# The stored expert weights: the two halves of each piece laid apart in DRAM

## The chip, the cores and the metric

The kernel runs on one core of a Trainium2 chip. The metric is device time in microseconds (us) of one execution. Five instruction streams take part: TensorE (PE, with its weight loads as PEld), VectorE (DVE), ScalarE (ACT), GpSimd (POOL) and SyncE (SP), which issues most DMA transfers. All transfers run on the same 16 DMA engines of the core, fed from several queues: q1 holds what SP issues, q10 what ACT issues, q0 the indirect transfers that POOL issues.

## The reference

```python
def _attn_ref(q, k, v, f_logit):        # (4, 8, 768, 48) each
    f = 1.0 / (1.0 + np.exp(-f_logit))
    for t in range(S):
        state = f[:, :, t, :, None] * state + np.einsum('bhd,bhe->bhde', k[:, :, t], v[:, :, t])
        y[:, :, t] = np.einsum('bhd,bhde->bhe', q[:, :, t], state)

def _moe_ref(x, w_in, w_out, alpha):    # x: 3072 x 384, hidden width 2048
    h = x @ w_in
    g = np.maximum(h, 0.0) + alpha * np.minimum(h, 0.0)
    return g @ w_out

def _moe2_ref(x, w_gate, w1, w2):       # 8 experts, 384 -> 1024 -> 384
    logits = x @ w_gate
    order = np.argsort(-logits.flatten())
    for idx in order:                   # greedy; every expert takes exactly 384 tokens
        tok, e = int(idx) // E, int(idx) % E
        if assigned[tok] >= 0 or counts[e] >= cap:
            continue
        assigned[tok] = e; counts[e] += 1
    for e in range(E):
        out[assigned == e] = np.maximum(x[assigned == e] @ w1[e], 0.0) @ w2[e]
```

The three run one after the other on 3072 tokens of width 384.

## The kernel before

**Matmuls in two parts.** Each fp32 operand of the two feed-forward layers is split into a rounded high part (fp32r) and the remainder, also fp32r. A product is three matmuls: high by low, low by high, high by high.

**Stages.** Attention runs in 24 chunks of 128 tokens; the first feed-forward layer in eight blocks of 384 tokens, each three chunks behind the attention. A block's result, three 128 x 384 tiles, is stored to the DRAM tensor `x2d` (SP issues these stores, ACT those of the last block). Then comes routing: for each expert in turn a search on DVE and PE finds the threshold, `lists` makes the list of its 384 tokens, `gather` (line 1442) reads their rows from `x2d` with three indirect DMAs on POOL, PE transposes the rows, and `expert` (line 1456) computes. The search for expert p+1 is woven into the matmuls of expert p.

**The expert weights.** `convert` (line 1398) runs beside the first feed-forward layer. For each expert e and each of eight pieces i it loads 128 x 768 floats of `w1` or `w2`, and for each half u of the piece ACT writes the high part and DVE the remainder into a tile `w` of 128 x 2 x 384 (name `wtwo`, three buffers), which SP stores to the DRAM tensor `wd`: 128 stores of 384 KB. `expert_weights` (line 1425) loads an expert's eight pieces when the search has named it, one DMA of 768 KB each (128 partitions x 1536 floats), into the SBUF space of the first layer's weights. Loads for one expert go to the `win` tiles, for the next to the `wo` tiles.

**What sets the order.** All of this is recorded as operations in a `Plan`, and a list scheduler (`schedule`, line 326) places them: it takes the operation that can start earliest by its own costs, breaks ties by priority, and emits every engine's instructions in that order. An operation waits for the operations whose memory regions overlap with its own. A region is a box of partitions and byte ranges; `region` (line 574) keeps at most 32 separate runs and merges the finest dimension of what is over:

```python
    while outer and count > 32:
        s, n = outer.pop(0)
        span += s * (n - 1)
        count //= n
```

`touch` (line 252) makes a write depend on earlier writes that overlap, for `x2d`, the output and `wd`. In idle time of PE the scheduler sets matmuls of constants (line 1667), which keep PE's clock up.

**Names in the rows.** Recorded operations have line 210 (feed-forward activations also 230), the loads of `wd` line 1440. `early` are tiles of attention and conversion, `common` gathered rows and block results, `late` the routing's small tiles, `weights` the SBUF weights, `rounded` split activations. `common<-x2d,late` is a gather, `x2d<-common` a block's store, `wd<-early` a store of a split half, `weights<-wd` a load of a piece, `bank<-ident,common` a transpose of gathered rows.

Of the kernel before, what the change touches and what calls it, by code (L numbers as in the profile page):

```python
# [9 lines left out]
F32 = mybir.dt.float32  # L10
# [10 lines left out]
N, DM, DF = B * S, H * D, 2048  # L21
E, FE = 8, 1024
# [609 lines left out]
class Kernel:  # L632
# [765 lines left out]
    def convert(self):  # L1398

        nc = self.nc  # L1400
        for e in range(E):
            for i in range(8):
                if i < 4:
                    t = self.cv.tile([128, KD, 256], F32, name="wraw", bufs=2)
                    src = self.w1[e].rearrange("(c q) f -> q c f", q=128)[:, :, i * 256:(i + 1) * 256]
                    flat = t.rearrange("p c f -> p (c f)")
                else:
                    t = self.cv.tile([128, 2, DM], F32, name="wraw", bufs=2)
                    src = self.w2[e].rearrange("(c q) d -> q c d", q=128)[:, 2 * i - 8:2 * i - 6, :]
                    flat = t.rearrange("p u d -> p (u d)")  # L1410
                nc.sync.dma_start(t, src)
                for u in range(2):
                    w = self.cv.tile([128, 2, DM], F32R, name="wtwo", bufs=3)
                    part = flat[:, u * DM:(u + 1) * DM]
                    nc.scalar.activation(w[:, 0], part, AF.Copy)
                    nc.vector.tensor_tensor(w[:, 1], part, w[:, 0].bitcast(F32), OP.subtract)
                    nc.sync.dma_start(self.wd[e, i, :, u], w.bitcast(F32))

    def expert_tiles(self, p):

# [4 lines left out]
    def expert_weights(self, p, ei):  # L1425

        ts = self.expert_tiles(p)

        def source(i, r):
            return self.wd[ds(r, 1), i].rearrange("o q u s d -> q (o u) s d")  # L1430

        if not self.plan:
            r = self.nc.sync.value_load(ei[0:1, 0:1], min_val=0, max_val=E - 1)
            for i, t in enumerate(ts):
                self.nc.sync.dma_start(t.bitcast(F32), source(i, r))
            return
        reg = []
        get = self.plan.add(("sync",), lambda e, b: reg.append(e.value_load(b(ei[0:1, 0:1]), min_val=0, max_val=E - 1)), [], [ei], 100.0)
        for i, t in enumerate(ts):
            self.plan.add(("sync",), lambda e, b, i=i, t=t: e.dma_start(b(t.bitcast(F32)), source(i, reg[0])), [t], [self.wd], 60.0, 128 * 1536 * 4, [get])  # L1440

    def gather(self, idx):
        xg = [self.gw.tile([128, DM], F32, name="g", bufs=3) for a in range(3)]
# [192 lines left out]
    def main(self, ctx):  # L1636
        tc = self.tc
        with ExitStack() as es:
            cp = es.enter_context(tc.tile_pool(name="consts", bufs=1))
            dp = es.enter_context(tc.tile_pool(name="dram", bufs=1, space=DRAM))  # L1640
            self.x2d = dp.tile([N, DM], F32, name="x2d")
            self.wd = dp.tile([E, 8, 128, 2, 2, DM], F32, name="wd")
            self.banks = 3
            self.wide = False
            self.urgent, self.slack = 0.0, SLACK
            with ExitStack() as e1:
                pp = e1.enter_context(tc.tile_pool(name="psum", bufs=1, space=PSUM))
                banks = [pp.tile([128, 512], F32, name=f"bank{i}") for i in range(8)]
                plan = self.nc = self.plan = Plan(tc, banks, (self.x2d.tensor.name, self.out.tensor.name, self.wd.tensor.name))
                self.pp = plan.group(None)  # L1650
                self.xp = plan.group(plan.arena("rounded"))
                self.gw = plan.group(plan.arena("common"))
                early = plan.arena("early")
                self.ap = plan.group(early)
                self.sp = plan.group(early, self.ap)
                self.cv = plan.group(early, self.ap)
                raw = [plan.arena(f"raw{n}") for n in reversed(range(NF))][::-1]
                self.raw = [plan.group(a) for a in raw]
                self.wp = [plan.group(plan.arena(f"weights{n}", "right", raw[:n + 1])) for n in range(NF)]
                over = raw + [early]  # L1660
                self.tail = plan.group(plan.arena("hidden", over=over))
                late = plan.arena("late", over=over)
                self.rp = plan.group(late, bufs=2)
                self.ep = plan.group(late, self.rp)
                self.record(cp)
                idle = self.ones[:, None, :].to_broadcast([128, 4, 128])
                plan.filler = lambda e, k: e.matmul(banks[k], self.ones, idle, start=True, stop=True)
                plan.emit()
            self.nc, self.plan, self.wide = tc.nc, None, False
            bad = tc.nc.values_load(self.bad[0:1, 0:1], min_val=0, max_val=1)  # L1670
            with tc.If(bad > 0):
                self.general()
# [169 lines left out]
```

## Time and profile before

| | |
|---|---|
| median of 3 runs | 859.87 us (858.52 to 860.99) |
| the profiled execution | 861.39 us, its span 859.5 us |
| mean granted TensorE clock over the span | 0.984 |
| PE busy | 825.2 us (96%) |
| PEld, DVE, ACT, POOL busy | 88%, 66%, 41%, 14% |
| moved by DMA | 172.60 MB, mean 201 GB/s |
| `wd` stores | 128 of 384 KB, 3.6 us to landing (median) |
| `wd` loads | 64 of 768 KB, 5.6 us to landing (median) |

The span is the time from the first to the last instruction of the profiled execution. What lies around it, 861.39 - 859.5 = 1.9 us, is start and end. [...] PE is busy nearly throughout, so an average says little; the stretches have to be read one by one, looking for those in which PE stands still and what it stands still for.

### The profile page before, as it was taken

Reading aid. Unit: us, or ns where it says so; the run is one execution under the profiler, and the core shown is the slowest. Engines: PE = TensorE matmul, PEld = TensorE weight load, DVE = VectorE, ACT = ScalarE, POOL = GpSimd, SP = SyncE. Lnnn points to the kernel's source line nnn. Section 1 sums busy time; section 2 is a strip of 40 time slices with the busy share of each in tenths; the row PEclk is TensorE's granted clock in tenths of the full one; section 3 lists DMA queues with packets and bytes.
Section 4 is the critical chain, followed back from the end, with each engine's and each line's share of the span. In section 5 each row is a group of like instructions: output and inputs, shape, how many; then the busy total and the mean of one; then the engine's idle time right before and its main releaser. Section 6 shows DMA issues by size and latency. Waiting matters only on the chain. (4 is left out here: it accounts for less than half of the span.)

```text
span 859.5 us, 16037 instructions
## 1 busy us (share of the span) xinstructions
PE 825.2 (96%) x6123; PEld 760.2 (88%) x6123; DVE 563.2 (66%) x1301; ACT 349.8 (41%) x742; POOL 121.5 (14%) x112
## 2 busy tenths in 40 slices
PE   7899899999999999999999999998899999999995
PEld 3678789999999999999999999986788898999995
DVE  6898996966966966966866645555667557453220
ACT  2477676455455455455454433410112222212220
POOL 3232410200200200300100001000102212201211
PEclk9899999999999999999999999999899999999998
DMA  8995215789788788898887610007548865777400
GB/s 175 277 251 162 48 29 140 160 281 288 207 286 271 217 281 261 213 308 245 233 266 271 230 76 28 1 10 311 186 175 339 340 248 194 266 278 260 163 27 32
DMA packets 92789, 172.60 MB, mean 201 GB/s; under 512 B 31672, under 2 KB 61376, under 8 KB 92704
## 3 DMA queue, kind: packets, MB, share of 16 engines
q1 hardware_dynamic: 89056, 161.45, 59.1%
q0 software_dynamic: 3072, 9.44, 3.1%
q8 instruction: 50, 0.82, 0.4%
q10 hardware_dynamic: 576, 0.60, 0.2%
q14 instruction: 35, 0.29, 0.1%
HBM read 111.69 MB, written 59.77 MB: 199 GB/s over the span
## 5 line engine op out<-in xcount | busy, mean ns | idle before, releaser
L210 PE MATMUL bank<-rounded,weights 128*128 128x384 f32 (+1 forms) x1740 | 355.5, 345 | 1.4 <-POOL weights L210 1.1
L210 PE MATMUL bank<-weights,rounded 128*128 128x392 f32 (+1 forms) x1620 | 324.0, 344 | 1.5 <-DVE weights L210 0.6
L210 PEld LDWEIGHTS bank<-rounded,weights 128*128 128x128 f32 (+1 forms) x1740 | 303.1, 188 | 8.3 <-issue 2.5
L210 PEld LDWEIGHTS bank<-weights,rounded 128*128 128x128 f32 x1620 | 287.4, 188 | 4.6 <-issue 1.3
L210 ACT ACTIVATE rounded<-bank 128x384 fp32r<-128x384 f32 x110 | 53.9, 491 | 193.9 <-PE bank L210 179.7
L210 DVE TENSOR_TENSOR early<-early 128x384 fp32r<-128x384 f32 (+2 forms) x196 | 119.3, 625 | 11.4 <-ACT early L210 10.9
L210 PEld LDWEIGHTS bank<-early 128*64 128x64 f32 (+2 forms) x1696 | 99.4, 156 | 22.7 <-issue 9.7
L210 PE MATMUL bank<-early 128*64 128x128 f32 (+3 forms) x1696 | 112.0, 272 | 3.7 <-ACT early L210 1.8
L210 DVE SCALAR_TENSOR_TENSOR common<-common,rest,bank 128x384 f32<-128x384 f32 x128 | 77.8, 608 | 52.0 <-ACT common L230 51.6
L210 POOL TENSOR_TENSOR rounded<-common,rounded 128x384 fp32r<-128x384 f32 x35 | 48.1, 1376 | 419.0 <-ACT rounded L210 380.2
L210 ACT ACTIVATE early<-early 128x384 fp32r<-128x384 f32 (+2 forms) x177 | 94.1, 545 | 30.0 <-DMA wd<-early 17.0
L230 ACT ACTIVATE common<-bank 128x384 f32<-128x384 f32 x128 | 62.5, 488 | 85.4 <-PE bank L210 85.2
L210 ACT ACTIVATE rounded<-common 128x384 fp32r<-128x384 f32 x118 | 61.7, 523 | 66.2 <-DVE common L210 66.1
L210 DVE TENSOR_TENSOR rounded<-common,rounded 128x384 fp32r<-128x384 f32 x83 | 47.6, 574 | 30.4 <-ACT rounded L210 22.0
L210 DVE SCALAR_TENSOR_TENSOR rounded<-bank,rounded 128x384 fp32r<-128x384 f32 x62 | 34.5, 556 | 50.3 <-ACT rounded L210 48.9
L210 DVE TENSOR_TENSOR_SCAN early<-early 128x516 f32<-128x516 f32 x48 | 62.7, 1306 | 2.5 <-ACT early L210 2.5
L210 ACT ACTIVATE common<-bank 128x384 f32<-128x384 f32 x48 | 23.2, 491 | 73.3 <-PE bank L210 68.0
L210 POOL DMA_INDIRECT out_dram<-common,late x24 | 24.6, 1023 | 168.9 <-ACT common L210 113.6
L210 DVE TENSOR_TENSOR late<-late,cols 128x1536 bf16<-128x1536 bf16 (+3 forms) x53 | 42.6, 817 | 0.2
L210 POOL DMA_INDIRECT common<-x2d,late x24 | 25.8, 1076 | 97.0 <-DMA weights<-wd 63.8
L210 DVE TENSOR_TENSOR rounded<-bank,rounded 128x384 fp32r<-128x384 f32 x48 | 26.3, 552 | 12.7 <-ACT rounded L210 12.5
L210 DVE TENSOR_TENSOR early<-bank,mask 128x512 f32<-128x512 f32 x48 | 31.3, 684 | 4.7 <-PE bank L210 4.5
(110 smaller groups left out, 499.3 us busy)
## 6 DMA issues: line engine op xcount, KB each, us to landing
wd<-early SPq DMA_DIRECT2D x128, 384.0 KB, 3.6
weights<-wd SPq DMA_DIRECT2D x64, 768.0 KB, 5.6
early<-in_w_dram SPq DMA_DIRECT2D x64, 384.0 KB, 4.4
early<-in_fkq_dram SPq DMA_DIRECT2D x46, 288.0 KB, 4.6
raw<-in_w_in_dram SPq DMA_DIRECT2D x16, 384.0 KB, 9.1
raw<-in_w_out_dram SPq DMA_DIRECT2D x16, 384.0 KB, 7.4
early<-in_v_dram SPq DMA_DIRECT2D x24, 192.0 KB, 3.4
x2d<-common SPq DMA_DIRECT2D x21, 192.0 KB, 2.8
```

The source lines that it names most:

```text
L210: op = self.add(engines, lambda e, b: getattr(e, method)(*[b(x) for x in a], **{n: b(x) for n, x in k.items()}), outs, ins)
L230: return e.activation(b(out), b(x), AF.Relu, scale=-1.0)
```

## The change

The DRAM tensor `wd` gets the half u outside the partition: `[e, i, u, 128, 2, 384]` where it was `[e, i, 128, u, 2, 384]`. A store of one half writes the same 128 runs of 3 KB, which now follow each other in DRAM, where they lay 6 KB apart. A load of a piece reads, for each partition, two runs of 3 KB that lie 384 KB apart, where it read one run of 6 KB; in SBUF the piece is laid out as it was. No instruction of any engine computes anything else.

```diff
@@ convert
-                    nc.sync.dma_start(self.wd[e, i, :, u], w.bitcast(F32))
+                    nc.sync.dma_start(self.wd[e, i, u], w.bitcast(F32))
@@ expert_weights
         def source(i, r):
-            return self.wd[ds(r, 1), i].rearrange("o q u s d -> q (o u) s d")
+            return self.wd[ds(r, 1), i].rearrange("o u q s d -> q (o u) (s d)")
...
             for i, t in enumerate(ts):
-                self.nc.sync.dma_start(t.bitcast(F32), source(i, r))
+                self.nc.sync.dma_start(t.bitcast(F32).rearrange("p u s d -> p u (s d)"), source(i, r))
...
         for i, t in enumerate(ts):
-            self.plan.add(("sync",), lambda e, b, i=i, t=t: e.dma_start(b(t.bitcast(F32)), source(i, reg[0])), [t], [self.wd], 60.0, 128 * 1536 * 4, [get])
+            self.plan.add(("sync",), lambda e, b, i=i, t=t: e.dma_start(b(t.bitcast(F32).rearrange("p u s d -> p u (s d)")), source(i, reg[0])), [t], [self.wd], 60.0, 128 * 1536 * 4, [get])
@@ main
-            self.wd = dp.tile([E, 8, 128, 2, 2, DM], F32, name="wd")
+            self.wd = dp.tile([E, 8, 2, 128, 2, DM], F32, name="wd")
```

The scheduler also sees the change. Before, one half's region was 128 runs at a pitch of 6 KB, more than 32, so it was merged into one range that covered the other half as well: the second store of a piece counted as a write over the first and was planned for after the first one's landing. Now the halves are two ranges that do not meet, and this link is gone for the 64 pieces. No semaphore wait stood for it in the program. The order on each engine moves from the first stores of `wd` to the end of the attention; four splits of feed-forward activations go from DVE to POOL; from the end of the attention on PE has the same instructions in the same order, apart from PSUM bank numbers.

On SP, where the conversion ends, the rows of before are these (the last two triples of `x2d` stores that SP issues are blocks 5 and 6; line 1438 reads the first expert's number):

```order
L210 DMA x2d<-common 128x384 x3
L210 DMA wd<-early 128x768 x2
...
L210 DMA early<-in_w_dram 128x2x384
L210 DMA wd<-early 128x768 x5
L210 DMA x2d<-common 128x384 x3
L1438 TENSOR_LOAD late
L1438 ISA x2
L1440 ISA
L1440 DMA weights_403<-wd 128x1536
L1440 ISA
L1440 DMA weights_591<-wd 128x1536
```

The same place in the changed program:

```order
L210 DMA wd<-early 128x768
L210 DMA x2d<-common 128x384 x2
L210 DMA wd<-early 128x768 x2
L210 DMA early<-in_v_dram 128x8x48
L210 DMA wd<-early 128x768
L210 DMA x2d<-common 128x384 x3
L1438 TENSOR_LOAD late
L1438 ISA x2
L1440 ISA
L1440 DMA weights_403<-wd 128x2x768
L1440 ISA
L1440 DMA weights_591<-wd 128x2x768
```

Between the stores of block 5 and those of block 6 stood 15 `wd` stores and now stand 3; each of the blocks before them had 21 to 24 and now has 24 to 27. The loads stand where they stood, each with two runs a partition.

On ACT, in the first such block, the rows of before (`early<-early` 128x384 is the high part of a half of `convert`, `common<-bank` at line 230 and `rounded<-common` are the feed-forward activation):

```order
L230 ACTIVATE common<-bank_71 128x384
L210 ACTIVATE rounded<-common 128x384
L210 ACTIVATE early<-early 128x384 x2
L230 ACTIVATE common<-bank_72 128x384
L210 ACTIVATE rounded<-common 128x384
L210 ACTIVATE early<-early 128x384 x2
L210 ACTIVATE common<-bank_68 128x384
```

And with the change:

```order
L230 ACTIVATE common<-bank_71 128x384
L210 ACTIVATE rounded<-common 128x384
L210 ACTIVATE early<-early 128x384
L230 ACTIVATE common<-bank_72 128x384
L210 ACTIVATE early<-early 128x384
L210 ACTIVATE rounded<-common 128x384
L210 ACTIVATE early<-early 128x384
L210 ACTIVATE common<-bank_68 128x384
L210 ACTIVATE early<-early 128x384
L210 ACTIVATE common<-bank_69 128x384
```

The halves no longer come in pairs but singly, each between two other activations.

## Rows read from the trace of the kernel before

**Rows 1.** Windows by stage: busy us (instructions) by engine, clock, DMA share, GB/s.

```profile
core 0: us, PE busy (x) PEld busy (x) DVE busy (x) ACT busy (x) POOL busy (x), PEclk, DMA share, GB/s
150.00:500.00 350.00, 349.76 (x2700) 335.93 (x2697) 257.16 (x472) 176.70 (x371) 29.81 (x21) 1.00 0.81 251
...
582.00:640.00 58.00, 50.97 (x389) 42.32 (x388) 32.84 (x118) 7.37 (x15) 6.45 (x6) 0.91 0.63 245
640.00:860.00 220.00, 208.39 (x1487) 197.28 (x1485) 101.88 (x348) 48.61 (x99) 43.94 (x42) 0.98 0.57 211
```

**Rows 2.** Waits of PE, 580 to 860 us: total us, times, longest.

```profile
PE bank L210 <- DMA common<-x2d,late: 7.0, 3, 4.9
```

**Rows 3.** Timeline 590 to 604 us: start, us, instruction, [idle before <- releaser].

```profile
591.84 0.33 SPq L1440 DMA_DIRECT2D weights<-wd  x1
...
592.75 0.34 ACTq L210 DMA_DIRECT2D x2d<-common  x1
...
599.30 0.23 DVE L210 SCALAR_TENSOR_TENSOR late<-bank,turn,late 128x8 f32<-128x8 f32 x1
600.78 1.12 POOL L210 DMA_INDIRECT common<-x2d,late  x1 [63.75 <-DMA weights<-wd]
...
603.95 0.47 PE L210 MATMUL bank<-ident,common 128*128 128x128 f32 x1 [4.95 <-DMA common<-x2d,late]
```

**Rows 4.** DMA packets from 592 to 596 us; share of 16 engines in that stretch.

```profile
DMA packets 305, 1.68 MB, mean 419 GB/s; under 512 B 32, under 2 KB 32, under 8 KB 305
...
q1 hardware_dynamic: 305, 1.68, 100.5%
```

**Rows 5.** DMA packets from 596 to 599.5 us, the same columns.

```profile
DMA packets 384, 1.47 MB, mean 421 GB/s; under 512 B 48, under 2 KB 176, under 8 KB 384
...
q1 hardware_dynamic: 240, 1.28, 87.7%
q10 hardware_dynamic: 144, 0.20, 15.2%
```

**Rows 6.** Windows after an earlier ACT store of x2d, issued at 572.95.

```profile
572.95:573.50 0.55, 0.55 (x6) 0.40 (x5) 0.08 (x1) 0.00 (x0) 0.00 (x0) 1.00 0.00 0
573.50:574.00 0.50, 0.50 (x4) 0.50 (x4) 0.50 (x3) 0.00 (x0) 0.00 (x0) 1.00 0.40 136
```

**Rows 7.** Transfers of the tile common: the stores of x2d that SP issues.

```profile
DMA to landing us min/median/max: 2.3/2.8/3.0
```

**Rows 8.** Timeline 613 to 645 us: the second expert's loads and gather.

```profile
613.42 31.12 SPq L1440 DMA_DIRECT2D weights<-wd  x12
...
620.70 1.52 POOL L210 DMA_INDIRECT common<-x2d,late  x1 [16.28 <-DVE rounded L210]
...
627.98 0.55 PE L210 MATMUL bank<-ident,common 128*128 128x128 f32 x3 [0.43 <-DMA common<-x2d,late]
...
630.95 0.90 PE L210 MATMUL bank<-ident,common 128*128 128x128 f32 x3 [1.60 <-DMA common<-x2d,late]
```

**Rows 9.** Windows of 2 us around the two falls of the clock, columns as in rows 1.

```profile
602.00:604.00 2.00, 0.06 (x1) 0.06 (x1) 0.00 (x0) 0.00 (x0) 1.49 (x2) 0.84 0.48 120
...
610.00:612.00 2.00, 2.00 (x13) 1.84 (x13) 0.41 (x3) 0.07 (x1) 0.00 (x0) 0.95 0.00 0
...
630.00:632.00 2.00, 1.05 (x5) 1.05 (x6) 0.52 (x1) 0.11 (x1) 0.00 (x0) 0.67 0.87 352
632.00:634.00 2.00, 2.00 (x9) 1.91 (x8) 0.71 (x2) 0.57 (x2) 0.00 (x0) 0.50 0.05 19
```

**Rows 10.** DMA from 150 to 500 us: queue q1, and the stores of wd.

```profile
q1 hardware_dynamic: 58039, 87.31, 80.9%
...
wd<-early SPq DMA_DIRECT2D x125, 384.0 KB, 3.6
```

**Rows 11.** Waits of ACT, 150 to 500 us: total us, times, longest.

```profile
ACT common L230 <- PE bank L210: 65.6, 60, 3.4
...
ACT early L210 <- DMA wd<-early: 17.0, 25, 2.4
```

## The prediction

> **What bounds the kernel now.** I read the windows by stage first. From 150 to 500 us, while the first feed-forward layer runs and the conversion stores `wd`, PE is busy for 349.76 of 350.00 us at full clock [rows 1]: TensorE sets the time there, and DMA, ACT and DVE lie behind it. From 582 to 640 us, where routing begins and the first two experts' weights are loaded, PE is busy for 50.97 of 58.00 us and the granted clock is 0.91 [rows 1]: this is the one stretch in which `wd` traffic could matter. From 640 us on it is 208.39 of 220.00 us, much of the rest being the drain at the end. The list of PE's waits says what it stands still for: gathered rows, 7.0 us in 3 waits, one of 4.9 us [rows 2]. That is its only row with a DMA; PE never waits for a weight load.
>
> The timeline shows the long wait [rows 3]. ACT issues the last block's last store of `x2d` at 592.75. The first gather, which reads `x2d`, starts at 600.78, and PE goes on at 603.95 after 4.95 us of idling. The page puts POOL's wait down to a weight load that landed about then; by the code the gather needs the store and no load. The router stands still too: its DVE step ends at 599.30 + 0.23, and its next matmul is queued on PE behind the transposes. So a store of 192 KB takes 592.75 to 600.78 = 8.0 us until its reader starts, where other stores of its kind land in 2.3 to 3.0 us [rows 7].
>
> What holds it up is visible in the DMA rows. From 592 to 596 us the engines carry queue q1 alone, at 100.5% [rows 4]: eight weight loads were issued ahead. The store's queue q10 appears only after 596.0, at least 3.25 us after the issue; an earlier store, with no loads about, was not moving within 0.55 us of its issue and was in the 0.5 us after that [rows 6]. Then both queues share the engines until 599.5 [rows 5].
>
> **Price of a packet.** In rows 4, 305 - 32 = 273 packets of 6 KB take 100.5% of 4 x 16 = 64 engine-us: 235 ns each, the small ones counted in. In rows 5, 176 - 48 = 128 store packets of 1.5 KB take 15.2% of 56 engine-us: 66 ns. A 3 KB load packet isn't in the trace. It lies between half of 235 (118 ns) and twice 66 (133 ns); a line through both rows gives 123 ns, which I take. An engine's share of one load goes from 8 x 235 = 1.88 to 16 x 123 = 1.97 us, eight loads from 15.0 to 15.7 us (bounds +0.1 to +2.0).
>
> **What the change costs and gives, part by part.**
>
> *The loads themselves: 0 on the path.* From 640 us on some seven experts share 220 us [rows 1], about 31 us each, against 16 us of loads; the first expert's loads still fill most of the engines until 599.5 [rows 5] and are done ahead of the transposes at 603.95. Without that cover they would cost the 0.7 us each time. SP issues a load in 0.33 us [rows 3]; even at double that it stays below the 1.9 us in which the engines carry it.
>
> *The first gather: -1.4 us.* In rows 5, (240 - 32) load packets of 6 KB and 128 store packets move in the same 3.5 us. An engine's eight store packets alone need 8 x 66 = 0.53 us, so they don't go as a block: the engines turn between the queues packet by packet. Each store packet then waits behind one load packet, and half as large a load packet saves 8 x (235 - 123) = 0.9 us. The delay ahead of the first store packet is 3.25 - 0.75, about 2.5 us beyond the quiet store's, ten load packets an engine. If that backlog is a number of packets, it falls by 10 x 112 ns = 1.1 us; if it is a number of bytes, by nothing. I take the number, since the turn that rows 5 show is by packets too: the store lands 2.0 us earlier. The loads end 0.7 us later, and a gather that starts earlier meets their tail, for which I take off 0.6. Bounds: 0.9 - 0.6 = -0.3, and -2.0 without a tail. PE and the router behind it both move up, since both hang on the gather.
>
> *The second gather: -1.3 us.* It is issued at 620.70, amid the loads that begin at 613.42, and PE gets its rows at 627.98, 7.3 us later; for the first, which met idle engines, that took 603.95 - 600.78 = 3.2 us [rows 3, 8]. Of the 4.1 us between, at most 1 - 123/235 = 48% goes, 2.0 us; with alternation alone, by the store's shares (0.9 of 2.0), 0.9. PE waits there for 0.43 and 1.60 us, 2.03 in all, and can't gain more. I take 1.3 between the two; bounds -0.7 and -2.0.
>
> *The clock: -0.9 us.* [...] With 3.5 us of idling left the first fall stays; with 0.7 us of 2.03 left the second, I think, doesn't come. Bounds 0, and -2.6 with half of the first at its full price (1.7) added.
>
> *The conversion: 0.* Nothing is added to it; the link between the two stores of a piece goes, so 24 to 27 stores are planned to a block instead of 21 to 24. The cover is TensorE's 349.76 of 350.00 us. The DMA engines were 80.9% taken [rows 10]; a tenth more in the same time makes 89%. ACT waited for stores 25 times, 2.4 us at most, and had 65.6/60 = 1.1 us in hand before each feed-forward activation [rows 11]. Four splits on POOL instead of DVE lie in the same cover. That the conversion ends earlier gives nothing: 125 of its 128 stores lie before 500 us [rows 10], the other three before 150, and the first load comes after 582.
>
> **Sum.** -1.4 - 1.3 - 0.9 = -3.6 us. Against the profiled execution, 861.39 - 3.6 = 857.8; that execution is 1.5 us above the median of the runs shown, and on 859.87 the forecast is 856.3. Bounds: -0.3 - 0.7 = -1.0 gives 858.9, and -2.0 - 2.0 - 2.6 = -6.6 gives 853.3.
>
> **Rivals.**
>
> *No change, by turns that are no turns: 859.9.* If an engine emptied one queue's share of a transfer before it went to the next, the store would wait behind 1.88 us of load before and 1.97 us after, nothing would be gained, and the loads' 0.7 us is hidden. Rows 5 speak against it: block by block the eight packets of each engine would be gone in 0.53 us, and the store took over 3 us. Softer forms, a backlog in bytes and both falls of the clock left, end at 858.9, within 0.3% of before as well. [...]
>
> *Slower: the conversion catches TensorE, about 864.* ACT works in order, and a high part that waits for its buffer's store holds the activations behind it. Before, 2.4 us was the longest wait; with 1.1 us in hand it decides from about 3.5 us on. If the denser stores fill the DMA engines (89% is near), their 3.6 us to landing [rows 10] grow, SP's queue falls behind its plan, and attention inputs queue behind stores. If the 25 waits grow by half, 8.5 us, and half of that reaches TensorE, it costs 4 us: 863.9, or 860.3 with the gains kept in full. For it speaks that ACT already waits in one of five stores (25 of 125); against it, that PE shows no idling at all there.
>
> *Faster by more, 853 to 854:* the first fall of the clock is cut short as well. It is the lower bound above.
>
> **How the numbers follow.** The forecast with its terms between the bounds, at least 2.6 us gained, has 0.42; the larger gain 0.08; a gain too small to tell or none 0.36; the conversion in the way 0.14. About 0.3%, 2.6 us, is what a measurement of this kernel can tell from no change. So: faster 0.50, same 0.36, slower 0.14. The likeliest case gives 856.3. The range runs from the lower bound 853.3 to 860.9, which takes in no change and leaves out most of the slower case.
>
> **What the profile after would show.** Right: the first gather starts about 2 us earlier than 8.0 us after ACT's last store of `x2d`, PE's 4.95 us wait is near 3.5, its two waits in the second gather fall below 1 us in sum, and the second stretch at half clock is missing; q1 has 8,192 more packets. The 6 KB packets' 235 ns turn into 123 for 3 KB. Wrong: the store's packets again begin 3.25 us after the issue, or the waits keep their length; or PE shows idling from 150 to 500 us behind ACT, and ACT's waits for `wd` stores pass 3.5 us.

## The result and the profile after

The changed kernel takes 869.92 us (median of 4 runs, 867.72 to 872.32), beside 859.92 us for the kernel before on the same chip: a ratio of 1.0118, 95% interval 1.0079 to 1.0157. It is slower, on the side to which the prediction gave 0.14, and outside its range. The profiled execution took 867.72 us, its span 865.9 us.

Read by stage, the windows of the changed kernel (busy us and instructions of PE, PEld, DVE, ACT and POOL, then clock, DMA share, GB/s, as in [rows 1]) show where the time went:

```profile
150.00:500.00 350.00, 343.45 (x2608) 326.35 (x2607) 252.80 (x459) 173.91 (x361) 33.04 (x24) 1.00 0.81 249
500.00:580.00 80.00, 79.47 (x468) 74.22 (x467) 40.12 (x94) 28.87 (x57) 2.54 (x2) 1.00 0.02 8
580.00:640.00 60.00, 53.94 (x430) 44.83 (x429) 35.15 (x131) 7.38 (x15) 6.44 (x6) 0.94 0.64 240
```

TensorE, full from 150 to 500 us before, now stands still there for 350.00 - 343.45 = 6.55 us, against 0.24 before. The waits of PE in that stretch (total us, times, longest) name feed-forward operands, and no DMA:

```profile
PE bank L210 <- DVE rounded L210: 5.2, 5, 2.1
PE bank L210 <- DVE early L210: 0.7, 1, 0.7
PE bank L210 <- POOL rounded L210: 0.7, 1, 0.7
```

The waits of ACT in the same stretch say what made these operands late; they answer to [rows 11]:

```profile
ACT early L210 <- DMA wd<-early: 58.9, 58, 3.4
...
ACT common L230 <- PE bank L210: 30.8, 31, 3.2
```

ACT's waits for `wd` stores grew from 17.0 to 58.9 us, by 41.9; the time in which it had waited for PE, its slack, shrank from 65.6 to 30.8, by 34.8. The difference, 7.1 us, is near the 6.3 us that PE lost; this is a rough account, since other waits of ACT moved too (for DVE ahead of splits from 51.1 to 47.3 us, for PE ahead of splits from 12.8 to 18.8). The list of DMA issues, as in [rows 10], has the cause of the waits: a store takes 5.3 us to landing instead of 3.6, while queue q1 moves no more than it did.

```profile
q1 hardware_dynamic: 57731, 86.72, 80.5%
...
wd<-early SPq DMA_DIRECT2D x125, 384.0 KB, 5.3
```

The longest of PE's waits, in the timeline (start, us, instruction, [idle before <- releaser]), shows the chain of one case:

```profile
466.17 0.53 ACT L210 ACTIVATE early<-early 128x384 fp32r<-128x384 f32 x1 [1.62 <-DMA wd<-early]
466.60 0.47 ACT L230 ACTIVATE common<-bank 128x384 f32<-128x384 f32 x1
...
467.20 0.61 DVE L210 SCALAR_TENSOR_TENSOR common<-common,rest,bank 128x384 f32<-128x384 f32 x1
467.51 0.52 ACT L210 ACTIVATE early<-early 128x384 fp32r<-128x384 f32 x1 [0.44 <-DMA wd<-early]
467.94 0.51 ACT L210 ACTIVATE rounded<-common 128x384 fp32r<-128x384 f32 x1
...
468.54 0.55 DVE L210 TENSOR_TENSOR rounded<-common,rounded 128x384 fp32r<-128x384 f32 x1
...
469.15 2.41 PE L210 MATMUL bank<-weights,rounded 128*128 128x392 f32 x9 [2.10 <-DVE rounded L210]
```

A high part (`early<-early`) stands ahead of the activation on ACT and waits 1.62 us for its buffer's store; the activation starts 0.43 us after the high part did, with no wait of its own left; a second high part, ahead of the split, waits another 0.44 us; then come the split and its remainder, and PE starts 2.10 us late. The other PE waits of 0.4 to 1.4 us that name DVE likewise follow ACT waits of 1.6 to 2.3 us for stores, while the longest such wait of the stage has no idle time of PE behind it:

```profile
447.24 0.53 ACT L210 ACTIVATE early<-early 128x384 fp32r<-128x384 f32 x1 [3.38 <-DMA wd<-early]
```

One wait is of another kind: the 0.7 us behind POOL follows no wait for a store, but one of ACT for an attention input (2.9 us), and 0.2 us of it are left in the half-stores kernel below. Behind the wait of 2.10 us the granted clock fell as well, to 0.50 (from 471 to 473 us). Windows of 2 us:

```profile
470.00:472.00 2.00, 2.00 (x10) 1.55 (x10) 0.88 (x3) 1.53 (x4) 0.00 (x0) 0.56 0.71 188
472.00:474.00 2.00, 2.00 (x21) 1.78 (x17) 0.57 (x2) 0.54 (x2) 0.00 (x0) 0.58 1.02 398
```

Below full clock lie (0.44 + 0.42) x 2 x 2 = 3.4 us at 0.50, worth, by estimate, up to half of that, 1.7. Lost PE time 6.3 and up to 1.7 for the clock make 8.0 us; the last store of `x2d` is issued at 600.62 instead of 592.75 [rows 3], 7.9 us later. That the two agree so well is in part luck: in the first 150 us the mean clock was 0.97 in the execution before and 0.99 in this one. From an event on, from the first block's last store of `x2d` (at 143.96 before, 141.01 after) to the last block's, it takes 459.6 us, 9.2 more than the 450.4 of the half-stores kernel below, which has the same order; some 1.2 us of that is in neither term. Either way the loss lies ahead of the part of the program for which the prediction was worked out: from the last store of `x2d` to the end of the span it takes 265.3 us, beside 266.7 before.

In that part the changes are small. The first gather, in the timeline, beside [rows 3]:

```profile
600.62 0.34 ACTq L210 DMA_DIRECT2D x2d<-common  x1
...
607.38 1.12 POOL L210 DMA_INDIRECT common<-x2d,late  x1 [62.40 <-DMA weights<-wd]
...
611.71 0.90 PE L210 MATMUL bank<-ident,common 128*128 128x128 f32 x3 [4.83 <-DMA common<-x2d,late]
```

From the store to the gather it takes 6.76 us (8.03 before), yet from the store to PE's next matmul 11.09 (11.20 before): the gather itself now takes 4.33 us instead of 3.17. The packets show which part of the store became quicker. From 600 to 604 us there is q1 alone (first all packets, then queue, packets, MB, share):

```profile
DMA packets 559, 1.62 MB, mean 405 GB/s; under 512 B 32, under 2 KB 32, under 8 KB 559
...
q1 hardware_dynamic: 559, 1.62, 103.6%
```

From 604.5 to 607 us both queues share the engines:

```profile
DMA packets 428, 1.02 MB, mean 410 GB/s; under 512 B 42, under 2 KB 147, under 8 KB 428
...
q1 hardware_dynamic: 307, 0.86, 86.8%
q10 hardware_dynamic: 121, 0.16, 17.5%
```

A 3 KB packet takes 103.6% of 64 engine-us over 559 - 32 = 527 packets, 126 ns with the small ones counted in; 123 was forecast. (A share over 100% means that packets of one engine overlap in the records.) The store's packets begin at least 604 - 600.62 = 3.4 us after the issue; by the packets' own times in the traces, the first starts 3.53 us after it, and 3.50 before, although the packets ahead of it are half as large. Once begun, 147 - 42 = 105 of its 128 packets lie in this stretch. From the first of the 128 to the last it is 1.6 us, where it was 2.8 before.

In the second gather PE waits for 1.17 us in one piece, where it waited 0.43 and 1.60 [rows 8], and the second fall of the clock is not there:

```profile
637.30 0.55 PE L210 MATMUL bank<-ident,common 128*128 128x128 f32 x3 [1.17 <-DMA common<-x2d,late]
```

```profile
600.00:620.00 20.00, 15.11 (x113) 9.65 (x112) 8.23 (x32) 2.46 (x5) 3.03 (x3) 0.83 0.57 211
620.00:640.00 20.00, 18.83 (x162) 17.00 (x162) 15.12 (x53) 3.94 (x8) 3.42 (x3) 1.00 0.91 343
```

### The profile page after: what moved, and what is told of

It reads as the page before. It is cut to its first block, busy times and chain, and to the rows that moved or that the text cites. A ratio compares the mean times of both kernels' runs of the same rounds, so it can differ in the third digit from the quotient of the medians.

```text
span 865.9 us, 16050 instructions
## 1 busy us (share of the span) xinstructions
PE 824.2 (95%) x6123; PEld 756.5 (87%) x6123; DVE 563.9 (65%) x1297; ACT 351.5 (41%) x742; POOL 127.0 (15%) x116
## 3 DMA queue, kind: packets, MB, share of 16 engines
q1 hardware_dynamic: 97248, 161.45, 59.5%
## 5 line engine op out<-in xcount | busy, mean ns | idle before, releaser
L210 DVE TENSOR_TENSOR early<-early 128x384 fp32r<-128x384 f32 (+2 forms) x196 | 122.1, 636 | 48.0 <-ACT early L210 47.3
L210 ACT ACTIVATE early<-early 128x384 fp32r<-128x384 f32 (+2 forms) x177 | 96.0, 550 | 72.2 <-DMA wd<-early 58.9
L210 POOL TENSOR_TENSOR rounded<-common,rounded 128x384 fp32r<-128x384 f32 x39 | 53.5, 1372 | 423.0 <-ACT rounded L210 390.9
L210 DVE TENSOR_TENSOR rounded<-common,rounded 128x384 fp32r<-128x384 f32 x79 | 45.4, 574 | 28.6 <-ACT rounded L210 22.7
```

The costliest lines, as they stand in the source:

```text
L210: op = self.add(engines, lambda e, b: getattr(e, method)(*[b(x) for x in a], **{n: b(x) for n, x in k.items()}), outs, ins)
```

## The experiments

The change does two things: it alters the layout in DRAM, and, through the regions that the scheduler sees, the order. The theory (order): the denser order makes the stores land later than planned, ACT is held by them, and TensorE behind it. The rival (layout): the stores' runs, no longer 6 KB apart, or the loads' 3 KB runs cost the time. Every ratio below is to the kernel before, run on the same chip in the same series; the chips differ (last section), so spans are compared within a series only.

### One part at a time

The layout alone: the changed kernel, with the lost link given back to the scheduler. Its order is that of the kernel before.

```diff
-                    nc.sync.dma_start(self.wd[e, i, u], w.bitcast(F32))
+                    put = nc.sync.dma_start(self.wd[e, i, u], w.bitcast(F32)); u and put.deps.add(first); first = put
```

> The changed layout of wd with the order of before: the scheduler is told that the second half's store follows the first, and every engine has the rows of before, but for the two runs in each load. Theory O (the order costs the time: denser conversion, ACT held by buffers whose stores haven't landed): ACT's waits for wd stores stay near 17 us, PE has no idling from 150 to 500 us, and what is left is the tail, where before took 276.8 us from the first weight load to the end and the change 275.4: about 1.4 us faster than before, ratio 0.997 to 1.000. Rival L (the layout costs it: 3 KB runs that follow each other in DRAM are written more slowly, so stores land in 5.3 us instead of 3.6): stores land in about 5 us in this order too, ACT waits some 50 us, and the ratio is 1.008 to 1.016 as with the whole change.

The order alone: the kernel before, its layout kept, with the link taken from the scheduler.

```diff
-                    nc.sync.dma_start(self.wd[e, i, :, u], w.bitcast(F32))
+                    put = nc.sync.dma_start(self.wd[e, i, :, u], w.bitcast(F32)); u and put.deps.discard(first); first = put
```

> The layout of before with the order of the change: the scheduler's link between the two stores of a piece is taken out, and every engine has the rows of the change, but for loads of one run of 6 KB. Theory O: as slow as the change up to the first weight load, with ACT's waits for wd stores at 50 to 65 us, stores that land in about 5 us and PE idling some 6 us from 150 to 500; without the gain of the tail the ratio is 1.010 to 1.020. Rival L: stores land in about 3.6 us, ACT waits near 17 us, ratio 0.998 to 1.003.

Measured: the layout alone 854.87 us, ratio 0.9981 (0.9957 to 1.0006); the order alone 866.44 us, ratio 1.0107 (1.0080 to 1.0133). The order carries the whole loss. The window from 150 to 500 us and ACT's wait for stores in it, first of the layout alone:

```profile
150.00:500.00 350.00, 349.78 (x2682) 335.96 (x2677) 256.32 (x472) 176.84 (x369) 28.19 (x21) 1.00 0.80 250
```

```profile
ACT early L210 <- DMA wd<-early: 13.1, 20, 2.2
```

The same two of the order alone:

```profile
150.00:500.00 350.00, 344.26 (x2621) 327.91 (x2620) 253.09 (x461) 173.55 (x363) 32.85 (x24) 1.00 0.81 249
```

```profile
ACT early L210 <- DMA wd<-early: 55.8, 54, 2.7
```

Stores land after 3.6 us with the layout alone and after 4.9 with the order alone (medians of all 128), so the later landing, too, comes mainly with the order.

### The same order, smaller stores

That the order costs the time does not yet show that it does so through the landing. So the order of the changed kernel was kept, and the stores made half as large: only the high parts are stored, and the experts' tiles are filled with high parts of two pieces, so the low parts are left out of the experts. (`bytes` and `deps` keep the scheduler's plan as it was.)

```diff
-                    nc.vector.tensor_tensor(w[:, 1], part, w[:, 0].bitcast(F32), OP.subtract)
-                    nc.sync.dma_start(self.wd[e, i, u], w.bitcast(F32))
+                    low = nc.vector.tensor_tensor(w[:, 1], part, w[:, 0].bitcast(F32), OP.subtract)
+                    put = nc.sync.dma_start(self.wd[e, i, u], w[:, 0].bitcast(F32)); put.bytes *= 2; put.deps.add(low)
...
-            return self.wd[ds(r, 1), i].rearrange("o u q s d -> q (o u) (s d)")
+            j = min(i, 6); return self.wd[ds(r, 1), j:j + 2].rearrange("o v u q d -> q (o v u) d")
...
-            self.wd = dp.tile([E, 8, 2, 128, 2, DM], F32, name="wd")
+            self.wd = dp.tile([E, 8, 2, 128, DM], F32, name="wd")
```

> The order of the changed kernel, instruction for instruction on TensorE, DVE, ACT and POOL; the wd stores carry only the high parts, 192 KB instead of 384, and the experts' loads (as many bytes as before, in runs of 1.5 KB) fill their tiles with high parts of two pieces, so the low parts are left out of the experts. Theory (the stores' landing time holds ACT, and through it TensorE): stores land in 3.5 us or less (5.3 in the changed kernel), ACT's waits for them fall from 58.9 us to under 25, TensorE is busy again for over 349 of 350 us from 150 to 500 us, and the time is 856 to 860, within 0.3% of before. Rival (the denser order as such, its splits on POOL and its engine queues, holds TensorE whatever the stores take): TensorE loses 4 us or more again and the time is over 865.

Measured: 861.39 us, ratio 1.0029 (1.0010 to 1.0049), a little over the 856 to 860 expected. The stores land after 3.7 us, ACT waits 9.0 us for them, and PE is full again, with its instructions in the changed kernel's order; window, wait and landing:

```profile
150.00:500.00 350.00, 349.55 (x2659) 334.80 (x2658) 255.42 (x465) 173.21 (x367) 32.83 (x24) 1.00 0.65 179
```

```profile
ACT early L210 <- DMA wd<-early: 9.0, 11, 2.4
```

```profile
wd<-early SPq DMA_DIRECT2D x125, 192.0 KB, 3.7
```

So it is the stores' time, not the order's rows as such, that holds TensorE. That stores land later because they stand closer is inferred; half as many bytes in the same order end it. Of the 0.3% that is left, the profiled executions show the place: from the first gather to the end of the span it takes 857.8 - 597.86 = 259.9 us, 3.1 more than the layout alone on the same chip (256.8, last section). There this kernel's loads have runs of 1.5 KB and its experts other data; that was not taken apart.

### An order that counts on the landing

The scheduler counts 1 us from the end of a transfer's bytes to its landing; for a `wd` store with nothing ahead of it, its plan has 0.65 us to the first byte, 1.3 for the bytes and this 1.0, some 3.0 us (lines 415 and 416 of the kernel). In the changed kernel, more was counted for the `wd` stores (2000.0 in ns; then 1000.0 and 4000.0 in the same place):

```diff
-                    nc.sync.dma_start(self.wd[e, i, u], w.bitcast(F32))
+                    nc.sync.dma_start(self.wd[e, i, u], w.bitcast(F32)).extra = 2000.0
```

> The change, but the scheduler counts 2.0 us more for a wd store until its landing, so that the buffer of a half is planned to be free later and the conversion is spread: 18 to 22 stores to a block instead of 24 to 27, the last 22 beside block 6's stores. Theory O: ACT's waits for stores fall below those of before (under 17 us), PE's idling from 150 to 500 us goes, and with the tail's gain the ratio to before is 0.996 to 1.000. Rival L: the layout slows stores in any order; they land in about 5 us, and the ratio stays above 1.005.

> The changed layout, with 1 us instead of 2 us more counted to the landing of a wd store. Theory (ACT's waits for the stores, set by landing beyond plan, hold the activations; the time follows their sum beyond the slack): the sum of ACT's waits for wd stores lies between 5.1 us (2 us more) and 58.9 us (none), some 20 to 30 us, TensorE loses 0 to 2 us from 150 to 500 us, and the time is between 854.5 and 860. Rival (the loss comes from the linkless order as such, whatever the waits): over 864 still. Waits above 40 us with a time below 857 would speak against the theory as well.

> The changed layout, with 4 us more counted to the landing of a wd store, twice that of the run with the later landing. Theory: ACT's waits are below 6 us and TensorE is full from 150 to 500 us; what can be lost is at the end of the conversion. If the last wd store is issued before some 545 us, the time is 853.5 to 856; if it comes later than some 550 us, the last block's hidden tiles wait for the arena as in the run with link and later landing, and the time is over 865. Rival (every further relief of ACT gains): below 853.

And 2 us together with the link of the layout alone:

```diff
-                    nc.sync.dma_start(self.wd[e, i, u], w.bitcast(F32))
+                    put = nc.sync.dma_start(self.wd[e, i, u], w.bitcast(F32)); u and put.deps.add(first); first = put; put.extra = 2000.0
```

> The changed layout with the scheduler's link of before and 2.0 us more to a store's landing: 15 to 20 stores to a block, 23 left for the last block, so the thinnest conversion that still ends ahead of routing. Theory O: hardly any ACT wait for stores (under 8 us), no idling of PE to 500 us; TensorE sets the time there, so no gain on the layout with the order of before: ratio 0.996 to 1.001. If conversion work now falls beside the last block and the search, DVE and ACT may be late for those: then up to 1.005. Rival L: above 1.005 from slower stores.

| counted more | ACT's waits for `wd` stores, 150 to 500 us | PE busy in 350 us | stores land | last `wd` stores issued | ratio |
|---|---|---|---|---|---|
| 0 (the change) | 58.9 us in 58, longest 3.4 | 343.45 | 5.3 us | 479.64 us | 1.0118 (1.0079 to 1.0157) |
| 1 us | 20.6 us in 27, longest 1.8 | 349.75 | 5.2 us | 489.27 + 7.4 us | 1.0012 (0.9996 to 1.0028) |
| 2 us | 5.1 us in 7, longest 1.7 | 349.76 | 4.4 us | 512.74 + 9.5 us | 0.9974 (0.9953 to 0.9995) |
| 4 us | none | 349.76 | 4.3 us | 577.66 + 7.9 us | 1.0487 (1.0470 to 1.0505) |
| 2 us and the link | 2.0 us in 2, longest 1.0 | 349.43 | 3.3 us | 572.61 + 7.6 us | 1.0387 (1.0359 to 1.0416) |

(The last stores stand in the timeline as one row of five, with its start and length.) The second row is the telling one. Its lines, from 150 to 500 us:

```profile
150.00:500.00 350.00, 349.75 (x2679) 336.24 (x2676) 256.62 (x466) 176.90 (x371) 36.55 (x26) 1.00 0.81 250
```

```profile
ACT early L210 <- DMA wd<-early: 20.6, 27, 1.8
```

```profile
wd<-early SPq DMA_DIRECT2D x125, 384.0 KB, 5.2
```

The stores land as late as in the changed kernel (5.2 us, 5.3 there), but the order counts on it, and PE loses nothing in this stretch (busy for 349.75 of 350.00 us). Here landing hurt by what it exceeded the plan, not by its length. (The ratio is 0.3% above the layout alone's; that was not taken apart.) The last two rows show the other end, and how: the stores spread until they reach past the attention. For 2 us with the link at most 1.005 had been expected, so its 1.0387 was a miss. The waits with 4 us counted, from 500 to 640 us:

```profile
PE bank L210 <- ACT hidden L210: 36.2, 1, 36.2
...
ACT hidden L210 <- DMA wd<-early: 3.1, 1, 3.1
```

The last block's hidden tiles (`hidden`) wait for the conversion's last stores, and PE waits 36.2 us for them. With the link PE's wait of this kind is 28.2 us. Both kernels lie over 30 us behind, and in both the last `wd` stores were issued after 570 us. That the hidden tiles lie in the conversion's space is read from the code.

### What the layout is worth

The later-landing order was also run with the layout of before, from the kernel before:

```diff
-                    nc.sync.dma_start(self.wd[e, i, :, u], w.bitcast(F32))
+                    put = nc.sync.dma_start(self.wd[e, i, :, u], w.bitcast(F32)); put.extra = 2000.0; u and put.deps.discard(first); first = put
```

And the layout was split once more, high and low part apart, in the order of before, so that loads and stores have runs of 1.5 KB (from the layout alone; store and loads are rearranged to match):

```diff
...
-            self.wd = dp.tile([E, 8, 2, 128, 2, DM], F32, name="wd")
+            self.wd = dp.tile([E, 8, 2, 2, 128, DM], F32, name="wd")
```

> The order of the run with the later landing, instruction for instruction, with the two halves of a piece together in DRAM as before (6 KB runs in the loads). It tells what the layout is worth with the order held. Theory (the layout shortens the second gather and keeps the clock from its second fall, some 1.6 us; the order does the rest): near 856.1, ratio 0.999, ACT waits for wd stores of 5 to 10 us as with the later landing, TensorE full from 150 to 500 us, the second fall of the clock present, 8.0 to 8.3 us from the last store of x2d to the first gather, 11.2 us from that store to TensorE's next matmul. Rival (the layout gives nothing, the order all): 854.4, no different from the run with the later landing.

> The layout split once more, so that high and low part lie apart too: loads and wd stores move runs of 1.5 KB; the order is that of the kernel before. Theory (the loads' backlog ahead of a store is time, not packets; the store's own packets alternate with the loads'; what the store gains is lost in the gather, whose packets wait for the loads' end): from the last store of x2d to the first gather 6.0 to 6.6 us (6.6 with 3 KB, 8.0 with 6 KB), its first packets still some 3.5 to 4 us after the issue, from the store to TensorE's next matmul again about 11.2 us; the time as with 3 KB, 853.5 to 856.5, ratio 0.996 to 1.0, TensorE full from 150 to 500 us. Rival (backlog counted in packets): the store's packets begin 2 to 2.5 us after the issue, and TensorE goes on 1 us or more earlier. Rival (smaller runs clog the conversion): ACT's waits for wd stores above 40 us, and 858 or more.

The first came out at 860.27 us, ratio 1.0026 (1.0012 to 1.0041), where 0.999 was expected, which made the layout worth 0.5% where the layout alone had shown 0.2%; so three kernels were repeated on one chip:

> The layout alone, in the order of the kernel before, once more on the chip of the following two, since the two later-landing runs with either layout were made on different chips. Theory (layout worth 1.6 us): ratio 0.998, and the gap between the two runs that follow is the same 0.2%. Rival (layout worth 4 to 5 us, as the ratios 0.9974 and 1.0026 of the later-landing order say): ratio 0.995.

> The changed layout with 2 us more counted to the landing, on the same chip as the layout alone and as the later landing with the old layout. Theory (order of later landing and order of before are worth the same, the layout 1.6 us): ratio 0.998, as the layout alone. Rival (this order is itself better than before's): below 0.9965.

> The later-landing order with 6 KB runs, on the same chip. Theory (layout worth 1.6 us, this order as good as before's): ratio 1.000, 0.002 above the run with 3 KB runs. Rival (layout worth 4 to 5 us): ratio 1.0026 again, 0.005 above the run with 3 KB runs.

Measured: 0.9982 (0.9964 to 0.9999) for the layout alone, 0.9985 (0.9969 to 1.0001) for the later landing, 1.0031 (1.0009 to 1.0052) for the later landing with the old layout. The layout's worth in the order of before stands at 0.19 and 0.18%, some 1.6 us. In the later-landing order it is 0.9985 / 1.0031 = 0.9954, 0.46%, again more; the two intervals (0.9969 to 1.0001 and 1.0009 to 1.0052) leave room for 0.1 to 0.8%. Why the old layout should cost more there isn't settled: PE is full from 150 to 500 us with either (busy for 349.75 and 349.76 of 350.00 us with the old layout, 349.76 and 349.75 with the new). In the second series a part is probably not the layout's: six of the old layout's twelve executions had a mean granted clock of 0.981 to 0.985 and took 862.4 to 866.0 us, the other six 0.987 to 0.991 and 859.2 to 861.4; and in the profiled one, of the first kind, the first block's last store of `x2d`, about when the `wd` stores begin, comes at 146.8 us instead of 142.8. The first series had the later landing slightly ahead of the layout alone (0.9974 to 0.9981), the second does not (0.9985 to 0.9982): both lie some 0.2% below the kernel before and over 1% below the change; the 0.2% is less than one measurement tells surely, and hangs on two series each.

The timelines of the first gather, from the last store of `x2d` (its issue) to POOL's gather and to PE's next matmul, and PE's waits for gathered rows from 500 us on (columns from each run's own trace):

| run | loads' runs | store to gather | store to PE | PE's waits for rows | clock, 580 to 640 us |
|---|---|---|---|---|---|
| before | 6 KB | 8.03 us | 11.20 us | 7.0 us | 0.91 |
| order alone | 6 KB | 8.29 | 11.54 | 8.5 | 0.91 |
| later landing, old layout, both series | 6 KB | 7.91, 8.05 | 11.16, 11.37 | 7.7, 7.4 | 0.94, 0.94 |
| the change | 3 KB | 6.76 | 11.09 | 6.0 | 0.94 |
| layout alone, both series | 3 KB | 6.60, 6.81 | 11.22, 11.14 | 6.1, 6.2 | 0.94, 0.94 |
| later landing, both series | 3 KB | 6.82, 6.59 | 11.23, 11.16 | 6.3, 6.2 | 0.94, 0.94 |
| 1.5 KB runs | 1.5 KB | 6.50 | 11.96 | 7.0 | 0.94 |

With 3 KB the gather starts 1.1 to 1.7 us earlier in every run, and PE goes on after the same 11.1 to 11.5 us as with 6 KB. With 1.5 KB (857.88 us, ratio 0.9993, 0.9981 to 1.0006) the store gains a little more and PE goes on later, after 11.96, where 11.2 was expected again. The packets of that run, from 595.4 to 598.4 us, the store having been issued at 595.26:

```profile
DMA packets 759, 1.12 MB, mean 373 GB/s; under 512 B 31, under 2 KB 759, under 8 KB 759
...
q1 hardware_dynamic: 759, 1.12, 106.5%
```

No packet of q10 for at least 3.1 us, and by the packets' times the first comes 3.80 us after the issue, where a backlog counted in packets would have made it 0.75 + 2.5 / 4 = 1.4 us by the prediction's reckoning. Behind packets of 6, 3 and 1.5 KB the store's first packet came after 3.50, 3.53 and 3.80 us, so what stood ahead of it in these runs was no fixed number of packets, but nearer a fixed time or number of bytes. A load packet of 1.5 KB takes 106.5% of 48 engine-us over 728 packets, 70 ns, so an engine's share of a load grows to 32 x 70 = 2.2 us.

The packets' times also tell what PE waits for at the first gather. With 6 KB, in all four executions, the gather's packets begin only as the last load packet ends (from 0.06 us ahead of its end to 0.33 behind), and PE goes on 3.2 to 3.3 us after the gather. With 3 and 1.5 KB, in all eight (the half stores and 1 us counted among them), the gather starts while loads still run. From the gather to PE it then takes anything from 4.1 to 5.5 us, but from the end of the last load packet to PE it takes 0.99 to 1.02 us each time. A finished transfer of the gather shows 16 packets of 4 bytes; at the loads' end 15 of them are there with 3 KB, and 15 for each of two transfers with 1.5 KB. Read as one such packet from each of the 16 engines, this makes one engine, still carrying loads, late.

## Why the prediction was wrong

**The conversion: 0.** This is the step that failed, and it set the sign. It read the cover from PE (349.76 of 350 us) and put the slack at 1.1 us ahead of each activation (the mean of the 60 that waited for PE) against the longest wait, 2.4 us; the rival was to decide "from about 3.5 us on". The longest wait after is 3.4 us, below that bound and without idle time of PE behind it, and PE lost 6.3 us all the same, behind waits of 1.6 to 2.3 us. What counts is how often the waits come and where: 58 instead of 25, in the case above one ahead of the activation and one ahead of its split, so that they add up against a slack that is there once. In sum the slack would have done, 65.6 us against 41.9 more of waiting; it did not lie where the waits fell. The rival's mechanism, ACT in order, a high part waiting for its buffer's store, the activation behind it, is shown by the order alone, by the half stores and by the landing counted in advance. Its price, 4 us, was mis-sized: 9.2 us in the order alone (1.07% of 859.9). It assumed that the waits grow by half; they grew to 3.5 times.

The reason for the longer landing was half right: stores that were planned one after the other now stand closer, 2.3 us apart instead of 2.7 (medians, 150 to 500 us), 128 of them from 143.78 to 479.64 us, where the last five of before began at 489.97. But the engines did not fill to the 89% that the prediction counted; q1 stayed at 80.5%. The warning was in [rows 11] and in the order's rows: halves that come singly, each ahead of an activation, on an engine that already waited in one of five stores. Those rows deserved more than 0.14.

**The loads: 0 on the path.** Right in its numbers (126 ns a packet, 123 forecast; q1 has 97,248 packets, 8,192 more), and in the tail; but the loads' end is what the first gather waits for, as the next step shows.

**The first gather: -1.4.** Its parts came out as follows. Alternation, -0.9: right, the store's packets move within 1.6 us instead of 2.8, and the gather starts 1.27 us earlier. Backlog counted in packets, -1.1: wrong; 3.50 us to the first packet with 6 KB, 3.53 with 3 KB, 3.80 with 1.5 KB. The tail, +0.6: too small; the gather takes 1.16 us longer and gives all of it back. In sum 11.20 became 11.09: -0.1. That the loads' end now sets PE's start is what the packets' times say (1.0 us from the one to the other in eight executions of six kernels, the later start with 1.5 KB among them); with 6 KB the gather itself set it, so the change moved the bound from the one to the other. Loads that are held back weren't tried.

An engine's eight store packets, each behind one load packet, would take 8 x (66 + 235) = 2.4 us with 6 KB, 8 x (66 + 126) = 1.5 with 3 KB and 8 x (66 + 70) = 1.1 with 1.5 KB; from the first store packet to the last it took 2.8, 1.6 and 1.1 us. So, by this reckoning, the engines turned between single packets of the trace. The no-change rival had an engine empty one queue's share of a transfer before it turns, which would have put the eight packets into 0.53 us; the 1.1 to 2.8 us measured are against it.

**The second gather: -1.3, and the clock: -0.9.** Right in mechanism: PE's waits there fell from 2.03 to 1.17 us, -0.9, at the end of the bounds (-0.7 to -2.0) where alternation acts alone; and the second fall of the clock is missing in the change and in every run with 3 KB (mean clock 0.94 from 580 to 640 us, against 0.91; it is missing, too, with the old layout in the later-landing order, so not by the layout alone). No run shows the 0.9 us for the clock by itself, nor the 1.7 in its bound: both are the author's estimates of what time at 0.50 costs. What the runs show is the clock: from 580 to 640 us its records have two stretches at 0.50 before, of 6.8 and 3.4 us, and one in the change, of 6.8. With the matmuls of constants in PE's gaps, from 592 to 598 us of before, PE is busy for 5.94 of 6.00 us and the clock is 1.00; no run leaves them out. The 0.9 us of PE's waits, the first gather's -0.1 and the prediction's 0.9 for the clock make -1.9 us, and the layout alone gained 1.6 (ratio 0.9982). So of the -3.6 us about half was there, beneath a loss of 9.2.

## What to carry to other kernels

An engine at 349.8 of 350 us does not prove cover: what feeds it may run on slack that a reordering eats. Before pricing a reordering at nothing, add up the waits of the in-order engine that feeds the bound one operand by operand, against the slack ahead of each; neither the longest single wait nor the slack of the whole stage says enough. And where a scheduler reads addresses, a change of layout is a change of order: run the two apart, and let the scheduler count the landing that the trace shows, but look at what the spread-out work still holds at its end.

## What was not expected of the hardware

- In these runs q10, started while the weight loads of q1 run, sees its first packet only after 3.4 to 3.6 us when these are in packets of 6 or 3 KB (ten executions), and after 3.8 with 1.5 KB (two); started with no loads about, in the kernel before, it sees it after 0.55 to 1 us [rows 6].
- The same program, the layout alone, on two chips: from an output's store on POOL to the next gather 2.26 us on one, 2.73 on the other, in four of the six such steps (all four kernels profiled on the one chip show 2.25 to 2.27 there, all others 2.73 to 2.80); from the first gather to the end of the span 851.6 - 597.73 = 253.9 and 855.3 - 598.48 = 256.8 us. That is more than the layout is worth. The rows, first of the one, then of the other:

```profile
671.14 0.97 POOL L210 DMA_INDIRECT out_dram<-common,late  x1 [13.93 <-ACT common L210]
673.40 0.99 POOL L210 DMA_INDIRECT common<-x2d,late  x1 [1.29 <-PE bank L210]
```

```profile
672.15 0.97 POOL L210 DMA_INDIRECT out_dram<-common,late  x1 [15.36 <-ACT common L210]
674.88 0.99 POOL L210 DMA_INDIRECT common<-x2d,late  x1 [1.77 <-PE bank L210]
```

- The mean granted clock of the first 150 us differs between executions, for the same program (later landing, old layout) 0.97 in the first series and 0.94 in the second, so a profile's times are compared from an event on, not from its start.
